# Network two, six steps of sevens: the read of the spare bank stands ahead of a gate, block 21 is bent later in one form of step, and a sum's split moves to the next step

## The chip, the cores and the metric

The kernel is one program on one core of a Trainium2 chip. The metric is the device time of one launch in microseconds (us); smaller is better. The kernel before takes 1674.57 us, the median of three runs between 1674.49 and 1675.16 us. The profile is one more execution, which took 1676.13 us; the trace of it covers a span of 1674.1 us.

## The reference

Three stages, all in float32: the real part of a two-dimensional Fourier transform of x (4 x 3072 x 256), a gated channel mix with squared ReLU (network one, 1024 hidden channels), and then network two, in which the change lies:

```python
def _moe2_ref(x, w_in, w_out):        # x: 12288 x 256, w_in: 256 x 2048, w_out: 2048 x 256
    h = x @ w_in
    g = h - np.tanh(h)
    return (g @ w_out).astype(np.float32)
```

## The kernel before, in words

**Precision.** TensorE multiplies a reduced float type here, so every operand is split into a high and a low part, and each product of a block is three matmuls (`mm3`, lines 395 to 397: high by high, high by low, low by high). The high part is a cast on ACT (`hi`, line 1082), the low part a subtraction (`lo`, line 1084) on DVE or on POOL.

**Tiling of network two.** The 12288 tokens are 12 passes of two token blocks of 512. The 2048 hidden channels are eight groups, q = 0 to 7, of two blocks of 128. One `step(n, q)` computes, for pass n and group q, the four blocks 11, 12, 21, 22 (128 x 512 each) of h, bends each (`bend`: tanh on ACT into a buffer `c`; then the "gate", a subtraction on DVE, gives g), and multiplies them by w_out. Pass 0 has another routine; passes 1 to 11 are 88 calls of `step`.

**Sevens.** The first matrix is done by seven products instead of eight for each step (the names a11, a12, s2, s3, s1, a22, s4 are the operands). They are accumulated in PSUM banks: X (two banks that alternate from step to step), Z, and W. Products that overlap in a bank are read off one after the other: Z begins as an ACT copy of X (line 1111, `z<-x` in the trace), takes a12, is bent and gated, then is overwritten by DVE with W plus the saved s3 (line 1191), bent by t22, gated (line 1208), and cast to the operand a22 (line 1082); X takes a22 at the end and is bent (t21). The second matrix is done by sevens too in the steps q = 0, 1, 3, 4, 6 and 7 (in pass 11 not in 7), and plainly, block by block, in q = 2 and 5. A step of sevens needs sums of its g blocks (s1, s2, s3, s4), which DVE and POOL make and which are split like the rest.

**The second matrix is late.** A step makes its operands while the next one or two steps run: `late(...)` runs pieces that the previous step (`p1`) left. What it can do depends on whether the previous step and the one before it were of sevens: form "b" if both were (q = 0, 1, 2, 5), "e" if only the previous was (q = 4, 7, and step (1,1)), "c" if the previous was not (q = 3, 6). So a pass runs b b b c e b c e.

**The spare bank.** Sums over several groups (a11, s1, s2, s3) are collected by `apart` in the bank X that this step does not use, called K; `add` then reads K on DVE into an accumulator `acc` in SBUF (lines 1028 and 1030). Two groups are read together where one follows the other. K is the previous step's X, so its first matmul comes after the last DVE read of that X (the low part of s1, `ls1`, line 1084 `s<-x,s`), and it is the next step's X, so the next step's first product comes after the read of K. Each step with a pair has two reads: one after the a11 cast, one (`k2`) after the gate of block 22.

**The order.** All engines run their instructions in program order; the order is the one in which `step` is written, and nothing else plans it. On ACT the tail of a step of form c or e stands as: tanh of Z (t22), tanh of X (t21, if the step is of sevens), cast of a22, and then, from the next step, the copy of block 22 to SBUF (`g22`, line 1235), the copy `z<-x`, and so on. Pass outputs of the pass before are made in steps 0, 1 and 3 by `part` (line 1045, DVE) and `whole_out` (line 1055, POOL). The stream of w_in (`TI`, 896 KB a step) and the stores go through SP's queue.

Of the kernel before, what the change touches and what calls it, by code (L numbers as in the profile page):

```python
# [406 lines left out]
class Kernel:  # L407
# [650 lines left out]
    def step(self, n, q):  # L1058

        V, A, T, G = self.V, self.A, self.T, self.G  # L1060
        TANH = mybir.ActivationFunctionType.Tanh
        S, W = self.S2[n], self.TI.pop(8 * n + q)
        p1, p2, p3 = self.pend, self.older, self.oldest
        seven = q in self.sevens(n)
        one, two = (bool(p and p["seven"]) for p in (p1, p2))
        form = "b" if one and two else "c" if not one else "e"
        group = lambda p, o: [o, p] if p["q"] in (1, 4, 7) else [p]
        def P(ps, k, start=False):
            i = RIGHT[k]
            mm3(T, ps, [W[:, 0, i], W[:, 1, i]], [S[k][:, 0], S[k][:, 1]], start)  # L1070
        def bend(src):
            t = self.room(self.act, "c", "c", 4)
            A.activation(t, src, TANH)  # L1073
            return t
# [4 lines left out]
        M, st = {}, {}  # L1079
        def hi(k, src):  # L1080
            M[k] = self.operand(k, *self.span(n, q, k))
            A.copy(M[k][:, 0], src)  # L1082
        def lo(k, src, eng):
            eng.tensor_sub(M[k][:, 1], src, M[k][:, 0].bitcast(F32))  # L1084
        late = lambda *names: [p1["late"][k]() for k in names]
# [12 lines left out]
        X, Z = self.bank(f"x{self.odd}", "x"), self.bank("z", "z")  # L1098
# [62 lines left out]
        add = k1() if k1 else nop  # L1161
# [15 lines left out]
        if not side:  # L1177
            lo("a11" if seven else "11", Z, V)
        if form == "b":
            late("hs2", "ls2")  # L1180
        elif form == "e":
            late("hs4", "ls4")
# [3 lines left out]
        add = k2() if k2 else nop  # L1186
# [5 lines left out]
        t22 = bend(Z)  # L1192
        if form == "b":
            late("hs4", "ls4")
        elif form == "e":
            late("hs2", "ls2")
        if q == 1 and n > 1:
            self.part(n - 1, 0, 1)
            self.whole_out(n - 1, 0, 1)
        if q == 0 and n > 1:  # L1200
            self.part(n - 1, 1, 0)
        if (n, q) == (1, 1):
            self.part(0, 0, 0)
        self.fill()
        if seven:
            P(X, "a22")
            st["t21"] = bend(X)
        V.tensor_sub(Z, Z, t22)  # L1208
        hi("a22" if seven else "22", Z)
        if seven and one:  # L1210
            V.tensor_sub(X, X, st["t21"])
        add()
        if (n, q) == (1, 1):
            self.part(0, 0, 1)
        if q == 1 and n > 1:
# [3 lines left out]
        if q == 3 and n > 1:  # L1219
            self.whole_out(n - 1, 1, 1)  # L1220
        self.fill()
        if not seven:
            P(X, "a22")
        P(Wb, "s4")
        def t21():
            st["t21"] = bend(X)
# [5 lines left out]
        if seven:  # L1232
            def f22():
                st["22"] = new("g22")
                A.copy(st["22"], Z)
            def g12():
                st["12"] = new("g12")
                V.tensor_sub(st["12"], Wb, st["t12"])
            def S4():
                st["12"] = new("g12")  # L1240
                V.tensor_sub(st["12"], Wb, st["22"])
            g = lambda k: st[k]
            do.update({
                "l22": lambda: lo("a22", Z, V), "f22": f22,
                "s3": lambda: V.tensor_sub(g("11"), g("11"), X), "s1": lambda: V.tensor_add(X, X, g("22")), "g12": g12,  # L1245
                "+s2": lambda: G.tensor_sub(g("22"), g("22"), g("11")), "+s4": lambda: G.tensor_sub(g("12"), g("12"), g("22")),  # L1246
                "G12": lambda: V.tensor_sub(Wb, Wb, st["t12"]), "S4": S4,
                "hs1": lambda: hi("s1", X), "ls1": lambda: lo("s1", X, V), "hs3": lambda: hi("s3", g("11")), "ls3": lambda: lo("s3", g("11"), G),
                "ha12": lambda: hi("a12", g("12") if "12" in st else Wb), "la12": lambda: lo("a12", g("12"), G), "LA12": lambda: lo("a12", Wb, V),
                "hs2": lambda: hi("s2", g("22")), "ls2": lambda: lo("s2", g("22"), G),  # L1250
                "hs4": lambda: hi("s4", g("12")), "ls4": lambda: lo("s4", g("12"), G)})
            w = self.W7[q]
        else:
            do.update(g12=lambda: V.tensor_sub(Wb, Wb, st["t12"]), h21=lambda: hi("21", X), l21=lambda: lo("21", X, V),
                      h12=lambda: hi("12", Wb), l12=lambda: lo("12", Wb, V))
            w = [[self.WO[q][:, s, 256 * c:256 * c + 256] for s in range(2)] for c in range(2)]
        self.oldest, self.older = p2, p1
        self.pend = dict(n=n, q=q, m=M, w=w, late=do, seven=seven)

# [4 lines left out]
    def phase2(self):  # L1264
        A, V = self.A, self.V
        z0 = 16 * NP
        self.W7, self.C, self.acc, self.older, self.oldest = {}, {}, {}, None, None
        self.at(z0 + 28, lambda: self.stream(8))
        self.TI = dict(enumerate(self.TI))
        for j in range(3, 8):  # L1270
            self.weights2(z0 + 4 * (j - 2), j, self.kp, "xt", 4)
        xt, wf, ring = (self.kp, "xt", 4), (self.p2a, "wf", 1), (self.w1, "T", 4)
        t4 = (lambda: self.p2b, lambda: self.p2a)
        for i, (q, slot, src) in enumerate(((0, 23, xt), (1, 26, xt), (3, 29, xt), (4, 38, wf), (6, 51, wf), (7, 56, wf))):
            self.seven(z0 + slot, q, *((self.p2a, f"TI{i}", 1) if i < 4 else ring), *src, t4[i % 2])
        for n in range(NP):
            for q in range(8):
                if n == 0 and q == 1:
                    self.xctx.close()
                    self.p2b = self.ctx.enter_context(self.tc.tile_pool(name="p2b", bufs=1, side="right", reuse_waits="tile"))  # L1280
                    self.homes = [[self.p2a, "WO0", 1, 1.5], [self.p2a, "WO1", 1, 2.5], [self.p2a, "WO3", 1, 4.5], [self.w1, "WR", 1, 0.], [self.p2b, "M", 2, 1.], [self.p2b, "M", 2, 1.1],
                                  [self.wvp, "wv", 4, 5.6], [self.wvp, "wv", 4, 7.6], [self.wvp, "wv", 4, 9.8]] + [[self.act, "m", 4, t] for t in (8.3, 8.6, 9.3, 9.8)]
                if q == 1 and n + 1 < NP:
                    u = self.left2(n + 1)
                    names = "a11 a12 a22 +s1 +s3 +s2 +s4 s1 s3 s2 s4".split()
                    when = (7, 8, 11, 12, 12, 15, 16, 16, 19, 20, 22) if n == 0 else (12, 12, 13, 14, 14, 15, 24, 24, 25, 26, 27)
                    self.at(z0 + 32 * n + (8 if n else 5), u["load"])
                    for k, name in zip(when, names):
                        self.at(z0 + 32 * n + k, u[name])
                if n:  # L1290
                    self.step(n, q)
                else:
                    w2 = [[self.WO[q][:, s, 256 * c:256 * c + 256] for s in range(2)] for c in range(2)]
                    self.quad(2, n, q, 8, self.S2[n], self.TI.pop(q), w2, None)
                if (n, q) == (NP - 1, 3):
                    self.at(self.now + 1, *self.plain(7))
            if n == 0:
                self.pend["seven"] = False
                self.C.update({(0, t, h): self.O[t][h] for t in range(2) for h in range(2)})
        p, w, n, G = self.pend, self.older, NP - 1, self.G  # L1300
        late = lambda *names: [p["late"][k]() for k in names]
        a11, h, s2, t = (self.acc[n, k] for k in ("a11", "h", "s2", "t"))
        self.direct(w, "a12")
        K = self.bank(f"x{1 - self.odd}", "k")
        L = self.bank("z", "l")
        def extra(ps, k):
            a, m = self.product(w, k)
            mm3(self.T, ps, a, [m[:, 0], m[:, 1]])
        extra(K, "s2")
        late("t21", "c12")  # L1310
        V.tensor_add(s2, s2, K)
        V.tensor_add(t, t, K)
        late("t12", "g21")
        G.tensor_add(s2, s2, h)
        self.whole(p, "11")
        extra(L, "s3")
        late("h21", "g12", "l21", "h12", "l12")
        V.tensor_add(t, t, L)
        self.whole(p, "22")
        G.tensor_add(h, h, t)  # L1320
        self.direct(w, "s4")
        V.tensor_add(t, t, a11)
        self.whole(p, "21")
        for k, (i, a) in enumerate((((1, 0), t), ((1, 1), h), ((0, 0), a11), ((0, 1), s2))):
            if k == 2:
                self.whole(p, "12")
            V.tensor_add(a, a, self.C.pop((n, *i)))
            self.send(n, *i, a, True)
# [118 lines left out]
```

## Time and profile before

| | |
|---|---|
| median of three runs | 1674.57 us (1674.49 to 1675.16) |
| profiled execution, device time | 1676.13 us |
| its span in the trace | 1674.1 us |
| PE (TensorE) busy | 1620.0 us, 97%, 7283 matmuls |
| DVE busy | 1356.0 us, 81% |
| ACT busy | 1273.7 us, 76% |
| POOL busy | 1112.9 us, 66% |
| network two, passes 1 to 11 | from about 742 us to the end |

A matmul here has a modelled end, so "busy" for PE says that the queue was full, and the count of matmuls in a stretch says how fast it ran. Idle time of an engine counts only where the engine that ends the stretch waits for it. In a row of the timeline the columns are: start (us from the span's start), duration, engine, line of the kernel, operation, output and inputs, shapes, and, in brackets, how long the engine had been idle before it and the instruction whose end released it.

### The profile page before, as it was taken

To read this page: it belongs to the slowest core of one execution; us is meant where nothing else is said; L and a number is where in the kernel's file an instruction comes from. 1 tells how busy PE (TensorE), PEld (TensorE's weight loads), DVE (VectorE), ACT (ScalarE), POOL (GpSimd) and SP (SyncE) were. 2 spreads that over 40 slices of the span, in tenths; PEclk is the share of its full clock that TensorE was granted. 3 is DMA by queue.
4 is the path that set the end of the run, shared out by engine and by line. 5 is a ranking of instruction groups with operands and counts; after the bars stand their busy time and mean duration, and the time that the engine had idled before them with its cause. 6 is when DMAs were issued, how large, how long until landed. Compare 5 with 4: busy or idle time off the path is not lost.

```text
span 1674.1 us, 22514 instructions
## 1 busy us (share of the span) xinstructions
PE 1620.0 (97%) x7283; PEld 1298.5 (78%) x7283; DVE 1356.0 (81%) x2115; ACT 1273.7 (76%) x2464; POOL 1112.9 (66%) x928
## 2 busy tenths in 40 slices
PE   8999999999999999999999999999999999999998
PEld 7978878888888887877777777777777777777776
DVE  7987888888888887777777777777787777778777
ACT  5987777777777777877878777777777777787774
POOL 1166667676666666768876767676767676767663
PEclk9999999999999999999999999999999999999999
DMA  9620111101111133443242424242424242424240
GB/s 333 169 58 26 46 45 64 34 30 57 53 57 63 45 107 105 160 159 143 73 134 93 132 95 132 95 132 95 133 94 133 91 136 89 139 88 138 89 141 26
DMA packets 59350, 168.76 MB, mean 101 GB/s; under 512 B 6864, under 2 KB 15824, under 8 KB 59232
## 3 DMA queue, kind: packets, MB, share of 16 engines
q1 hardware_dynamic: 57648, 162.87, 28.7%
q0 software_dynamic: 1440, 4.46, 1.6%
q8 instruction: 57, 0.93, 0.2%
q14 instruction: 61, 0.50, 0.1%
q10 hardware_dynamic: 144, 0.00, 0.0%
HBM read 128.43 MB, written 38.86 MB: 100 GB/s over the span
## 4 chain that ended last, share of the span: by engine, by line
PE 35%; ACT 10%; DVE 8%; issue 1%; DVEq 0%; POOLq 0%; ACTq 0%
PE x L395 4%; PE k L395 4%; PE k L397 3%; PE k L396 3%; PE x L397 3%; PE x L396 3%; ACT c L1073 3%; PE o L395 3%; PE o L397 3%; PE o L396 3%; ACT s L1082 3%; DVE a L1084 2%; ACT a L1082 2%; PE w L395 2%; PE w L397 1%; PE w L396 1%
## 5 line engine op out<-in xcount | busy, mean ns | idle before, releaser
L1084 POOL TENSOR_TENSOR s<-g,s 128x512 fp32r<-128x512 f32 x195 | 251.6, 1298 | 14.4 <-ACT s L1082 12.8
L1246 POOL TENSOR_TENSOR g<-g,g 128x512 f32<-128x512 f32 x107 | 138.6, 1296 | 118.8 <-DVE x L1245 73.2
L696 POOL TENSOR_TENSOR s<-xk,s 128x512 fp32r<-128x512 f32 x94 | 125.0, 1331 | 102.2 <-ACT s L694 97.7
L696 POOL TENSOR_TENSOR a<-xk,a 128x512 fp32r<-128x512 f32 x70 | 92.3, 1328 | 123.3 <-ACT a L694 123.2
L396 PE MATMUL o<-m,wv 128*128 128x512 f32 x384 | 149.6, 390 | 0.0
L397 PE MATMUL o<-m,wv 128*128 128x512 f32 x384 | 149.5, 389 | 0.0
L395 PE MATMUL o<-m,wv 128*128 128x512 f32 x384 | 149.5, 389 | 0.0
L1073 ACT ACTIVATE c<-z 128x512 f32<-128x512 f32 x176 | 105.3, 598 | 42.5 <-DVE z L1191 41.4
L1082 ACT CAST s<-g 128x512 fp32r<-128x512 f32 x195 | 120.8, 620 | 5.9 <-DVE g L1245 5.9
L1077 ACT COPY s<-x 128x512 f32<-128x512 f32 x176 | 103.9, 590 | 24.6 <-PE x L397 22.2
L1084 DVE TENSOR_TENSOR a<-z,a 128x512 fp32r<-128x512 f32 x108 | 74.3, 688 | 48.6 <-ACT a L1082 41.0
L571 ACT ACTIVATE c<-z 128x512 f32<-128x512 f32 x112 | 67.3, 601 | 54.8 <-DVE z L660 54.5
L578 DVE TENSOR_TENSOR m<-z,m 128x512 fp32r<-128x512 f32 x112 | 76.8, 686 | 33.4 <-ACT m L576 33.4
L1111 ACT COPY z<-x 128x512 f32<-128x512 f32 x88 | 50.2, 570 | 65.8 <-PE x L397 30.0
L1208 DVE TENSOR_TENSOR z<-z,c 128x512 f32<-128x512 f32 x88 | 61.6, 700 | 46.4 <-ACT c L1073 44.7
L395 PE MATMUL x<-a,TI 128*128 128x512 f32 x192 | 77.0, 401 | 17.2 <-DVE acc L1030 16.9
L430 POOL TENSOR_TENSOR xr<-xt,xr 128x512 fp32r<-128x512 f32 x46 | 60.5, 1322 | 48.3 <-ACT xr L429 48.3
L1084 POOL TENSOR_TENSOR a<-g,a 128x512 fp32r<-128x512 f32 x64 | 83.1, 1299 | 12.0 <-ACT a L1082 9.8
L576 ACT CAST m<-z 128x512 fp32r<-128x512 f32 x112 | 65.9, 589 | 29.9 <-DVE z L664 25.4
L396 PEld LDWEIGHTS o<-m,wv 128*128 128x128 f32 x384 | 72.1, 188 | 15.6 <-DVE m L578 0.5
L395 PEld LDWEIGHTS o<-m,wv 128*128 128x128 f32 x384 | 72.1, 188 | 15.2
L397 PEld LDWEIGHTS o<-m,wv 128*128 128x128 f32 x384 | 72.1, 188 | 15.1
(1020 smaller groups left out, 5824.6 us busy)
## 6 DMA issues: line engine op xcount, KB each, us to landing
TI<-ti SPq DMA_DIRECT2D x88, 896.0 KB, 4.8
spill<-r SPq DMA_DIRECT2D x48, 256.0 KB, 2.6
xk<-spill SPq DMA_DIRECT2D x48, 256.0 KB, 6.5
out<-o SPq DMA_DIRECT2D x44, 256.0 KB, 2.4
ti<-TI SPq DMA_DIRECT2D x8, 896.0 KB, 4.8
wf<-wf SPq DMA_DIRECT2D x17, 256.0 KB, 2.9
raw<-w_in SPq DMA_DIRECT2D x32, 128.0 KB, 2.2
cv<-w_out SPq DMA_DIRECT2D x16, 256.0 KB, 3.2
```

The costliest lines, as they stand in the source:

```text
L395: T.matmul(ps, w[0], m[0], start=start, stop=False, skip_group_check=True)
L396: T.matmul(ps, w[0], m[1], start=False, stop=False, skip_group_check=True)
L397: T.matmul(ps, w[1], m[0], start=False, stop=stop, skip_group_check=True)
L571: A.activation(t, src, ACT.Tanh if ph == 2 else ACT.Relu)
L576: A.copy(M[blk][:, 0], g)
L578: V.tensor_sub(M[blk][:, 1], g, M[blk][:, 0].bitcast(F32))
L696: eng.tensor_sub(S[name][:, 1], src(), S[name][:, 0].bitcast(F32))
L1073: A.activation(t, src, TANH)
L1077: A.copy(t, src)
L1082: A.copy(M[k][:, 0], src)
L1084: eng.tensor_sub(M[k][:, 1], src, M[k][:, 0].bitcast(F32))
L1246: "+s2": lambda: G.tensor_sub(g("22"), g("22"), g("11")), "+s4": lambda: G.tensor_sub(g("12"), g("12"), g("22")),
```

## The change

Four edits in `step` and what goes with it; the number of instructions on each engine stays the same.

1. The read of K (`add`, the second one of a step) stands ahead of the gate of block 22, and the pass outputs `part`/`whole_out` of steps 0 and 1, which stood ahead of that gate, stand behind the gates.
2. In form c, a step of sevens now runs its last product P(X, "a22") and the bend of block 21 after the cast of a22 (as plain steps do); in forms b and e the order of the two stays.
3. In form e the split of the previous step's sum s2 (`hs2` on ACT, `ls2` on POOL) is not run; it is kept in `self.slow`, and the next step, of form b, runs it just ahead of its own `hs2`, `ls2`. After the last step it is run at the beginning of the tail.
4. The loading of w_out's sevens for group 4 is set two slots later (40 for 38), once in the program.

```diff
         if form == "b":
+            if self.slow:
+                self.slow["late"]["hs2"]()
+                self.slow["late"]["ls2"]()
             late("hs2", "ls2")
         elif form == "e":
             late("hs4", "ls4")
...
         t22 = bend(Z)
         if form == "b":
             late("hs4", "ls4")
-        elif form == "e":
-            late("hs2", "ls2")
+        if (n, q) == (1, 1):
+            self.part(0, 0, 0)
+        self.fill()
+        early = seven and form != "c"
+        if early:
+            P(X, "a22")
+            st["t21"] = bend(X)
+        add()
+        V.tensor_sub(Z, Z, t22)
+        hi("a22" if seven else "22", Z)
+        if seven and one:
+            V.tensor_sub(X, X, st["t21"])
         if q == 1 and n > 1:
             self.part(n - 1, 0, 1)
             self.whole_out(n - 1, 0, 1)
         if q == 0 and n > 1:
             self.part(n - 1, 1, 0)
-        if (n, q) == (1, 1):
-            self.part(0, 0, 0)
-        self.fill()
-        if seven:
-            P(X, "a22")
-            st["t21"] = bend(X)
-        V.tensor_sub(Z, Z, t22)
-        hi("a22" if seven else "22", Z)
-        if seven and one:
-            V.tensor_sub(X, X, st["t21"])
-        add()
...
         self.fill()
-        if not seven:
+        if not early:
             P(X, "a22")
+            if seven:
+                st["t21"] = bend(X)
         P(Wb, "s4")
...
+        self.slow = p1 if form == "e" else None
         self.oldest, self.older = p2, p1
...
-        for i, (q, slot, src) in enumerate((... (4, 38, wf), ...)):
+        for i, (q, slot, src) in enumerate((... (4, 40, wf), ...)):
...
         a11, h, s2, t = (self.acc[n, k] for k in ("a11", "h", "s2", "t"))
+        self.slow["late"]["hs2"]()
+        self.slow["late"]["ls2"]()
         self.direct(w, "a12")
```

What the edits do to the order of the instructions is shown at four places. First, DVE at the end of a step of form c (pass 3, step 3); `z<-w,s` is line 1191 that overwrites Z, `z<-z,c` the gate of block 22, `acc<-k` the read of K, `a<-z,a` the low part of a22. Before:

```order
L1191 TENSOR_TENSOR z<-w,s 128x512
L1208 TENSOR_TENSOR z<-z,c 128x512
L1028 COPY acc<-k 128x512
L1084 TENSOR_TENSOR a_9499<-z,a_9499 128x512
L1228 TENSOR_TENSOR w<-w,s 128x512
L1231 TENSOR_TENSOR x<-x,c 128x512
```

and after:

```order
L1194 TENSOR_TENSOR z<-w,s 128x512
L1028 COPY acc<-k 128x512
L1206 TENSOR_TENSOR z<-z,c 128x512
L1084 TENSOR_TENSOR a_9496<-z,a_9496 128x512
L1232 TENSOR_TENSOR w<-w,s 128x512
L1235 TENSOR_TENSOR x<-x,c 128x512
```

The read of K and the gate have changed places; nothing else moved there on DVE.

Second, ACT at the same place and into the next step, of form e (pass 3, steps 3 and 4); `c<-z` is t22, `c<-x` is t21, `a<-z` the cast of a22, `g<-z` the copy of block 22. Before:

```order
L1073 ACTIVATE c<-z 128x512
L1073 ACTIVATE c<-x 128x512
L1082 CAST a_9499<-z 128x512
L1235 COPY g_9517<-z 128x512
L1111 COPY z<-x 128x512
L1073 ACTIVATE c<-w 128x512
```

and after:

```order
L1073 ACTIVATE c<-z 128x512
L1082 CAST a_9496<-z 128x512
L1073 ACTIVATE c<-x 128x512
L1239 COPY g_9517<-z 128x512
L1111 COPY z<-x 128x512
L1073 ACTIVATE c<-w 128x512
```

The tanh of X has moved behind the cast of a22.

Third, ACT at the end of a step of form e and the start of the next, of form b (pass 3, steps 4 and 5); `s_9584` is the high part of the second sum s2 of step 3. Before:

```order
L1082 CAST s_9571<-g_9551 128x512
L1073 ACTIVATE c<-z 128x512
L1082 CAST s_9584<-g_9517 128x512
L1073 ACTIVATE c<-x 128x512
L1082 CAST a_9593<-z 128x512
L1235 COPY g_9609<-z 128x512
L1111 COPY z<-x 128x512
```

and after, where the same cast has the name `s_9661` and stands later, in step 5 (the second piece):

```order
L1082 CAST s_9571<-g_9551 128x512
L1073 ACTIVATE c<-z 128x512
L1073 ACTIVATE c<-x 128x512
L1082 CAST a_9590<-z 128x512
L1239 COPY g_9606<-z 128x512
L1111 COPY z<-x 128x512
...
L1077 COPY s<-x 128x512
L1082 CAST s_9661<-g_9517 128x512
L1082 CAST s_9664<-g_9606 128x512
L1073 ACTIVATE c<-z 128x512
```

One cast has left the stretch between the tanh of Z and the tanh of X.

Fourth, DVE at the end of a step of form b (pass 7, step 0); `o<-acc,o` is the pass output of line 1045, `x<-x,c` the gate of block 21, `g<-g,x` the sum s3 of the next step. Before:

```order
L1191 TENSOR_TENSOR z<-w,s 128x512
L1045 TENSOR_TENSOR o<-acc,o_11628 128x512
L1208 TENSOR_TENSOR z<-z,c 128x512
L1211 TENSOR_TENSOR x<-x,c 128x512
L1030 TENSOR_TENSOR acc<-acc,k 128x512
L1084 TENSOR_TENSOR a_12414<-z,a_12414 128x512
L1245 TENSOR_TENSOR g_12382<-g_12382,x 128x512
```

and after:

```order
L1194 TENSOR_TENSOR z<-w,s 128x512
L1030 TENSOR_TENSOR acc<-acc,k 128x512
L1206 TENSOR_TENSOR z<-z,c 128x512
L1209 TENSOR_TENSOR x<-x,c 128x512
L1045 TENSOR_TENSOR o<-acc,o_11628 128x512
L1084 TENSOR_TENSOR a_12413<-z,a_12413 128x512
L1249 TENSOR_TENSOR g_12379<-g_12379,x 128x512
```

The read of K has gone from behind both gates to ahead of them, and the pass output from ahead of the gates to behind them.

## Rows read from the trace of the kernel before

**Rows 1.** The profile's first line.
```profile
span 1674.1 us, 22514 instructions
```

**Rows 2.** Windows: window, PE, PEld, DVE, ACT, POOL, PEclk, DMA, GB/s.
```profile
400.00:500.00 100.00, 100.00 (x441) 82.18 (x441) 88.89 (x131) 75.88 (x141) 68.11 (x55) 1.00 0.14 46
...
733.00:1650.00 917.00, 880.55 (x3712) 683.39 (x3710) 725.03 (x1127) 713.79 (x1336) 654.66 (x522) 1.00 0.33 111
```

**Rows 3.** Waits of PE, 742 to 1660: sum, count, longest (us).
```profile
PE x L395 <- DVE acc L1030: 16.9, 20, 1.3
PE z L395 <- ACT z L1111: 11.4, 23, 1.1
PE k L395 <- DVE s L1084: 6.7, 22, 1.8
```

**Rows 4.** Timeline, pass 5, end of step 3 (c) into step 4 (e).
```profile
1108.16 0.70 DVE L1208 TENSOR_TENSOR z<-z,c 128x512 f32<-128x512 f32 x1 [0.67 <-ACT c L1073]
...
1108.77 0.68 DVE L1028 COPY acc<-k 128x512 f32<-128x512 f32 x1
...
1110.19 0.60 ACT L1073 ACTIVATE c<-x 128x512 f32<-128x512 f32 x1 [2.07 <-PE x L397]
...
1110.68 0.58 ACT L1082 CAST a<-z 128x512 fp32r<-128x512 f32 x1
...
1111.07 0.39 PE L397 MATMUL x<-a,TI 128*128 128x512 f32 x1
...
1111.30 0.69 DVE L1084 TENSOR_TENSOR a<-z,a 128x512 fp32r<-128x512 f32 x1 [1.85 <-ACT a L1082]
...
1112.02 0.59 ACT L1235 COPY g<-z 128x512 f32<-128x512 f32 x1 [0.76 <-DVE a L1084]
...
1112.64 0.57 ACT L1111 COPY z<-x 128x512 f32<-128x512 f32 x1
...
1113.27 0.50 PE L395 MATMUL z<-a,TI 128*128 128x512 f32 x1 [0.45 <-ACT z L1111]
```

**Rows 5.** Timeline, pass 5, step 4 (e) into step 5 (b).
```profile
1117.12 0.19 PEld L395 LDWEIGHTS w<-s,TI 128*128 128x128 f32 x1 [0.30 <-DVE g L1241]
...
1119.42 0.61 ACT L1082 CAST s<-g 128x512 fp32r<-128x512 f32 x1
...
1119.55 0.70 DVE L1208 TENSOR_TENSOR z<-z,c 128x512 f32<-128x512 f32 x1 [0.66 <-ACT c L1073]
...
1120.41 0.59 ACT L1082 CAST a<-z 128x512 fp32r<-128x512 f32 x1
...
1121.52 0.69 DVE L1084 TENSOR_TENSOR a<-z,a 128x512 fp32r<-128x512 f32 x1 [0.27 <-ACT g L1235]
...
1124.82 0.50 PE L395 MATMUL k<-a,W 128*128 128x512 f32 x1 [0.24 <-DVE s L1084]
```

**Rows 6.** Timeline, pass 6, steps 0 to 1 to 2 (b).
```profile
1160.07 0.68 DVE L1045 TENSOR_TENSOR o<-acc,o 128x512 f32<-128x512 f32 x1
...
1160.28 2.56 POOL L1084 TENSOR_TENSOR s<-g,s 128x512 fp32r<-128x512 f32 x2
...
1163.17 0.68 DVE L1084 TENSOR_TENSOR a<-z,a 128x512 fp32r<-128x512 f32 x1
...
1163.31 0.50 PE L395 MATMUL x<-a,TI 128*128 128x512 f32 x1 [0.65 <-DVE acc L1030]
...
1164.30 0.57 ACT L1111 COPY z<-x 128x512 f32<-128x512 f32 x1 [1.40 <-PE x L397]
...
1165.20 1.30 POOL L1246 TENSOR_TENSOR g<-g,g 128x512 f32<-128x512 f32 x1 [2.37 <-DVE x L1245]
...
1165.93 0.69 DVE L1084 TENSOR_TENSOR s<-x,s 128x512 fp32r<-128x512 f32 x1 [0.28 <-ACT s L1082]
...
1166.84 0.40 PE L395 MATMUL k<-s,W 128*128 128x512 f32 x1
...
1177.70 0.40 PE L395 MATMUL k<-a,W 128*128 128x512 f32 x1
```

More of the change, by code (lines that the diff above doesn't have):

```diff
@@ L1266, in phase2 @@
         z0 = 16 * NP
-        self.W7, self.C, self.acc, self.older, self.oldest = {}, {}, {}, None, None
+        self.W7, self.C, self.acc, self.older, self.oldest, self.slow = {}, {}, {}, None, None, None
         self.at(z0 + 28, lambda: self.stream(8))
@@ L1273, in phase2 @@
         t4 = (lambda: self.p2b, lambda: self.p2a)
-        for i, (q, slot, src) in enumerate(((0, 23, xt), (1, 26, xt), (3, 29, xt), (4, 38, wf), (6, 51, wf), (7, 56, wf))):
+        for i, (q, slot, src) in enumerate(((0, 23, xt), (1, 26, xt), (3, 29, xt), (4, 40, wf), (6, 51, wf), (7, 56, wf))):
             self.seven(z0 + slot, q, *((self.p2a, f"TI{i}", 1) if i < 4 else ring), *src, t4[i % 2])
```

## The prediction

> **What bounds the kernel now.** I read the page's first line, then windows, then the waits of PE, and last the timeline at three places. The span is 1674.1 us [rows 1]; the device time of that execution is 1676.13, so 2.0 us lie outside the span and stay. The windows [rows 2] say how full TensorE is (granted clock 1.00 in both stretches, the level of 2.4 GHz): in a dense stretch of network one 441 matmuls pass in 100 us, 0.227 us each. In passes 1 to 11 of network two 3712 pass in 917 us; at 0.227 they would need 842. So TensorE waits there for up to 75 us, while DVE, ACT and POOL are busy for 725, 714 and 655 of the 917: no engine is full, the chains between them set the end. The list of waits [rows 3] names three kinds: X's first product waits for the read of K (16.9 us in 20), Z's first product for the copy `z<-x` (11.4 in 23), K's first product for the low part of s1 (6.7 in 22), 35.0 us together. The matmul that waited is listed with 0.50 us, the others with 0.39 [rows 4]: 0.11 of restart, 65 times, 7.2 us. So 42 us hang on the three waits, and each edit points at one of them.
>
> **c to e (edits 1 and 2 together).** In [rows 4] the gate of block 22 runs at 1108.16, the read of K behind it at 1108.77, but the cast of a22 only at 1110.68: ACT first bends X (t21, 1110.19), which waits for X's last product. Then follow one after the other the low part (1111.30), the copy of block 22 (1112.02), `z<-x` (1112.64), and Z's first product at 1113.27. It had 0.45 idle ahead of it; the matmul before it ended at 1112.82, so began at 1112.43, and 1112.65 was possible. After the change the gate comes a DVE slot later, at 1108.77, and ends at 1109.47 (0.70 as now); the cast starts at 1109.5, 1.17 earlier than now, since t21 no longer stands ahead of it. The low part follows at 1110.13 and the block's copy at 1110.86 (steps of 0.62 and 0.72, as in the rows). `z<-x` would follow at about 1111.50, when X's product is there (its last matmul runs from 1111.07 to 1111.46), and ends at 1112.07, ahead of 1112.65. So the wait goes, 0.62 and the restart. More hangs on this Z: the bend of block 11, its gate, the cast and low part of block 12 and the sum for which `w<-s` waited at 1117.12 [rows 5]. That comes about 1.0 earlier, at 1116.12.
>
> **e to b (edit 3).** Here K's first product waits for s1, at 1124.82 with 0.24 idle [rows 5]. Backwards its chain is the low part of a22 (1121.52, held by ACT's copy of block 22), the cast of a22 (1120.41), and ahead of it on ACT t21 and the cast of s2 (1119.42, 0.61 long). With Z's chain 1.0 earlier and that cast gone from ACT, the gate (1119.55 now, 1118.55 then) is what the cast of a22 waits for: 0.70 on, at 1119.25, 1.16 earlier. I carry 1.11 on, since ACT must first end t21: the low part comes at 1120.41 instead of 1121.52. What follows on DVE up to the low part of s1 moves with it, and K's first product starts at 1123.71, 1.11 earlier. That is all of what c to e gave and a little more, one gain for each c, e, b and not a sum of two. Of the 22 waits of K one lies in the tail; the 21 others get the gain in full (23.3 us). The first e, step (1,1), has no such wait behind it and pass 0's outputs in it; I give it 0.8. Together **24.1 us**.
>
> The cast and POOL's subtraction of s2 move into the next b step, 0.6 of ACT and 1.3 of POOL. There POOL stands idle 2.37 us ahead of its next sum (at 1165.20, [rows 6]), which hides it, and the products that use s2 come a step later. Behind pass 11 nothing hides it: the 1.2 that K's last wait loses is given back by 1.30 of POOL ahead of the tail's first s2. I take 0; from -1.3 to +1.3 is possible.
>
> **b to b to b (edit 1).** X's first product waits for the read of K (1163.31, 0.65 idle, [rows 6]); by [rows 3] the mean of the 20 is 0.85. The read moves ahead of the gate, so this wait goes. But DVE's work is the same five instructions: pass output (1160.07 to 1160.75), gate, block 21's gate, read of K, low part of a22 (1163.17). In the new order the read can start about where the pass output ends now, 1160.8; two gates and the pass output follow in slots of 0.6, and the low part is at 1163.2 as before. `z<-x`, which waited for X (1164.30), follows the low part's end, at 1163.9. Behind it ACT's casts of s3 and s1 wait for sums on DVE that have not moved, so that s1's low part comes at 1165.73 instead of 1165.93. K's first product, without a wait at 1166.84 now, would be reached by TensorE at 1165.9 and must wait for s1 till 1166.47, with 0.11 of restart. An x wait of 0.9 turns into a k wait, and 0.26 is gained. In the next step, by the same working, 1177.70 becomes 1177.13. I take 0.55 a pass, **5.5 us** in ten. The ends: 0 if s1 doesn't move, and 16.9 + 20 x 0.11 = 19 if K's product waits for nothing.
>
> In the plain steps 2 and 5 the gate, too, is a slot of 0.61 later; their operands are used behind other products, and the waits listed [rows 3] have none on them. I take 0; at most 21 x 0.61 = 13 are lost. The later load (edit 4) is once in the program, half a pass ahead of its use: 0.
>
> Sum: 24.1 + 5.5 = 29.6, so 1676.13 - 29.6 = 1646.5 for an execution like the profiled one; its time lies 1.56 over the median of the runs, so **1645.0** for the median.
>
> One row speaks on a danger of edits 1 and 3, POOL's subtractions and the pass output beside each other. In [rows 6] the pass output, whose inputs are both in SBUF (1160.07, 0.68), lies beside two subtractions of POOL (1160.28, 2.56 for both): DVE takes 0.68 as in its other rows and POOL 1.28 each. By that the move costs nothing. The Trainium skill ("SBUF — State Buffer", section "Who interferes with whom") has it that DVE and GpSimd share a pair of SBUF ports under an exclusive lock. By that rule such pairs would take longer, which these rows don't show; what it would make of the time is the fourth rival.
>
> **The rivals.**
> 1. The three waits vanish and none takes their place: 42 less, **1632**. For it: no engine is busy over 79% of the stretch. Against it: in b steps s1's low part hangs on DVE instructions in series that the change doesn't shorten. Chance 0.12.
> 2. The gains are given back at the next wait: in b to b all, and in c to e all but the cast of s2 that leaves ACT's path (0.61, [rows 5]), because `z<-x` is held by X or the next step by block 12. Then 22 x 0.61 = 13: **1661**. For it: the end of X's product leaves `z<-x` only 0.04 of slack. Against it: each link of Z's chain stands back to back in [rows 4]. Chance 0.17.
> 3. Slower: the later gate decides. In all 65 steps with a second read of K (0, 1, 2, 3, 5, 6 of a pass) the gate moves back by 0.61. If K's products end later than the bend t22, as they do once TensorE waits at K, the read stands, and the gate, the cast, the block's copy and the low part are late by as much, and with them the next step's Z and s1. 65 x 0.61 = 39.7 lost against 24.1 won: **1690**. It decides from the point where Z's chain, not the bend of X on ACT, is the last thing that the next step's s1 waits for, in c as in b. Against it: in c the cast stands 1.2 behind the gate's end now (twice a slot). Chance 0.06.
> 4. POOL and DVE hold each other up where the subtraction of s2 now lies: 23 x 1.30 = 30 lost against 29.6 won, **1675**. Against it the rows of 0.68 and 2.56 above. Chance 0.02.
>
> **How the numbers follow.** The forecast has 0.63, the rivals 0.12, 0.17, 0.06, 0.02. About 0.2%, 3.3 us, is what a measurement of this kernel can tell from no change. The forecast's own bounds go from 1631.5 (b to b 19 in place of 5.5) to 1659 (plain steps 13 and the tail 1.3 lost). With rivals 1 and 2 and their spread the range for 8 in 10 is 1631 to 1664; most of rivals 3 and 4 and the edges are left out. Faster by over 0.2%: the forecast and rivals 1 and 2, 0.92, less 0.01 of the second's tail: 0.91. No change: that 0.01 and rival 4, 0.03. Slower: 0.06.
>
> **What would show it.** In the trace after: no wait of X on the read of K worth 2 us in the list, waits of Z on `z<-x` under a third of 11.4; about 42 waits of K on s1 in place of 22, over 10 us in sum; in form c the cast of a22 right behind its gate and ahead of t21; K's first product in steps 1 and 2 a little over 10.8 apart, as now (1166.84 to 1177.70); POOL at 1.30 and DVE at 0.69 as before. The prediction is wrong if Z's waits stay at 11 us, if the cast of a22 in form c starts over 0.3 behind its gate's end, if the b steps come out longer, or if K's waits add up to as much as X's and Z's gave back.

## The result, and the profile after

The changed kernel takes 1648.32 us (median of four runs, 1647.95 to 1648.92) against 1674.53 for the kernel before in the same comparison: ratio 0.9844, 95% interval 0.9827 to 0.9861. That is 26.2 us, 1.56%. The forecast was 1645.0.

The profiled execution took 1648.92 us. The first line of its page, and its windows with the columns of [rows 2]:

```profile
span 1647.1 us, 22505 instructions
...
400.00:500.00 100.00, 100.00 (x442) 82.22 (x441) 88.87 (x131) 75.33 (x141) 68.16 (x54) 1.00 0.14 46
733.00:1625.00 892.00, 872.89 (x3720) 686.86 (x3719) 730.88 (x1132) 728.40 (x1341) 654.78 (x524) 1.00 0.34 114
```

The dense stretch of network one is the same, and the granted clock is. Network two now passes 3720 matmuls in 892 us where it passed 3712 in 917; at 0.227 us each they would need 844, so at most 48 us are not filled where it was 75.

The waits of PE after (sum, count, longest, in us), to be held against [rows 3]:

```profile
PE k L395 <- DVE s L1084: 6.4, 22, 1.4
PE o L396 <- POOL s L1084: 5.3, 10, 0.6
PE o L395 <- DVE o L1045: 4.5, 10, 0.7
PE z L395 <- ACT z L1111: 1.0, 1, 1.0
PE w L395 <- DVE g L1245: 0.9, 1, 0.9
PE k L396 <- POOL s L1084: 0.8, 1, 0.8
```

The 16.9 us of X behind the read of K are gone, and 22 of the 23 waits of Z. Two kinds are new in the list, 10 each: a product into an output bank (`o`) that waits for POOL's low part of a sum, and one that waits for the pass output of line 1045. The list leaves out waits of about 0.1 us and less, and one new kind is among these: K's first product in step 2 (below).

**c to e.** The timeline of the changed kernel where [rows 4] stood before (pass 5, end of step 3):

```profile
1097.31 0.69 DVE L1028 COPY acc<-k 128x512 f32<-128x512 f32 x1 [0.61 <-PE k L397]
...
1097.92 0.69 DVE L1206 TENSOR_TENSOR z<-z,c 128x512 f32<-128x512 f32 x1
...
1098.64 0.59 ACT L1082 CAST a<-z 128x512 fp32r<-128x512 f32 x1 [1.31 <-DVE z L1206]
...
1099.26 0.69 DVE L1084 TENSOR_TENSOR a<-z,a 128x512 fp32r<-128x512 f32 x1 [0.65 <-ACT a L1082]
...
1099.35 0.60 ACT L1073 ACTIVATE c<-x 128x512 f32<-128x512 f32 x1
...
1099.98 0.59 ACT L1239 COPY g<-z 128x512 f32<-128x512 f32 x1
...
1100.71 0.57 ACT L1111 COPY z<-x 128x512 f32<-128x512 f32 x1
...
1101.81 0.39 PE L395 MATMUL z<-a,TI 128*128 128x512 f32 x1
```

The gate comes a slot behind the read, the cast 0.72 after the gate's start, and the tanh of X behind the cast. Z's first product has 0.39, not 0.50, and no idle time: it waited for nothing.

**e to b.** Where [rows 5] stood (pass 5, steps 4 and 5):

```profile
1105.34 0.50 PE L395 MATMUL w<-s,TI 128*128 128x512 f32 x1
...
1107.76 0.70 DVE L1206 TENSOR_TENSOR z<-z,c 128x512 f32<-128x512 f32 x1 [0.67 <-ACT c L1073]
...
1108.49 0.59 ACT L1082 CAST a<-z 128x512 fp32r<-128x512 f32 x1 [0.18 <-DVE z L1206]
...
1109.60 0.69 DVE L1084 TENSOR_TENSOR a<-z,a 128x512 fp32r<-128x512 f32 x1 [0.54 <-ACT g L1239]
...
1112.90 0.50 PE L395 MATMUL k<-a,W 128*128 128x512 f32 x1 [0.24 <-DVE s L1084]
```

The cast waits for the gate now. From `w<-s` to the low part of a22 it is 4.26 us; before it was 1121.52 - 1117.12 = 4.40 [rows 5]. K still waits 0.24 for s1, earlier by all that its step won.

**b to b to b.** Where [rows 6] stood (pass 6, steps 0 to 2):

```profile
1147.22 3.79 POOL L1084 TENSOR_TENSOR s<-g,s 128x512 fp32r<-128x512 f32 x3
...
1149.57 0.68 DVE L1045 TENSOR_TENSOR o<-acc,o 128x512 f32<-128x512 f32 x1
...
1150.17 0.68 DVE L1084 TENSOR_TENSOR a<-z,a 128x512 fp32r<-128x512 f32 x1
...
1151.07 0.50 PE L396 MATMUL o<-s,W 128*128 128x512 f32 x1 [0.51 <-POOL s L1084]
...
1153.74 0.39 PE L395 MATMUL k<-s,W 128*128 128x512 f32 x1
...
1161.12 0.47 PE L395 MATMUL o<-s,W 128*128 128x512 f32 x1 [0.42 <-DVE o L1045]
...
1164.18 0.19 PEld L395 LDWEIGHTS k<-a,W 128*128 128x128 f32 x1 [0.51 <-DVE s L1084]
...
1164.18 0.50 PE L395 MATMUL k<-a,W 128*128 128x512 f32 x1
```

The three subtractions of POOL in one row (the moved one is the first) end at 1151.01, and the second matmul of a direct product waits for the last of them. In the next step the first matmul of the same product waits for the pass output, which stands behind the gates now. Between the two, K's first product in step 1 waits for nothing (0.39). In step 2 it waits for the low part of s1: its weight load names it, the matmul has 0.50, and its idle time is 0.09. So it is in each of passes 2 to 11, which makes 32 waits of K on s1 where the list shows 22.

A table by step, made from the start of each `z<-x` copy to the next (mean of passes 2 to 11, us), shows where the time came from:

| from step | 0 | 1 | 2 | 3 (c to e) | 4 | 5 | 6 (c to e) | 7 | pass |
|---|---|---|---|---|---|---|---|---|---|
| before | 10.58 | 10.89 | 9.59 | 12.13 | 9.65 | 9.66 | 12.06 | 9.72 | 84.28 |
| after | 10.23 | 10.76 | 9.67 | 11.14 | 9.68 | 9.69 | 10.91 | 9.67 | 81.75 |

Two intervals give 2.1 of the 2.5 us of a pass, both from a c step into an e step.

### The profile page after: what moved, and what is told of

It is laid out like the page before. It is cut to its first block, busy times and chain, and to the rows that moved or that the text cites. A ratio compares the mean times of both kernels' runs of the same rounds, so it can differ in the third digit from the quotient of the medians.

```text
span 1647.1 us, 22505 instructions
## 1 busy us (share of the span) xinstructions
PE 1610.7 (98%) x7283; PEld 1301.4 (79%) x7283; DVE 1356.9 (82%) x2115; ACT 1285.9 (78%) x2464; POOL 1110.5 (67%) x928
## 4 chain that ended last, share of the span: by engine, by line
PE 35%; ACT 8%; DVE 7%; POOL 2%; issue 2%; DVEq 0%; POOLq 0%; ACTq 0%
PE k L395 3%; ACT s L1082 3%; PE o L396 3%; PE o L397 3%; PE o L395 3%; PE k L396 3%; PE k L397 3%; PE x L397 3%; PE x L395 3%; PE x L396 3%; PE w L395 2%; POOL s L1084 2%; DVE a L1084 2%; PE w L397 1%; PE w L396 1%
## 5 line engine op out<-in xcount | busy, mean ns | idle before, releaser
L1030 DVE TENSOR_TENSOR acc<-acc,k 128x512 f32<-128x512 f32 x86 | 59.1, 687 | 44.1 <-PE k L397 44.1
L576 ACT CAST m<-z 128x512 fp32r<-128x512 f32 x112 | 65.9, 589 | 27.5 <-DVE z L664 23.0
L1082 ACT CAST a<-z 128x512 fp32r<-128x512 f32 x108 | 64.0, 593 | 29.5 <-DVE z L1206 27.3
```

The lines of the kernel that those rows point to most:

```text
L576: A.copy(M[blk][:, 0], g)
```

## The experiments

All were run against the kernel before on one chip for each of three groups; ratios are to it. "Interval 3" is the column 3 of the table above, and differences of intervals are to the changed kernel, mean of passes 2 to 11.

| kernel | us, median | ratio, 95% interval |
|---|---|---|
| the change | 1648.32 | 0.9844 (0.9827 to 0.9861) |
| no_read | 1651.59 | 0.9859 (0.9846 to 0.9873) |
| no_late21 | 1669.20 | 0.9963 (0.9951 to 0.9976) |
| no_slow | 1648.73 | 0.9843 (0.9830 to 0.9856) |
| twice | 1679.42 | 1.0024 (1.0013 to 1.0034) |
| split_last | 1650.96 | 0.9853 (0.9833 to 0.9873) |
| outputs | 1647.24 | 0.9825 (0.9808 to 0.9843) |
| read_b_only | 1646.22 | 0.9822 (0.9806 to 0.9838) |
| three | 1644.19 | 0.9811 (0.9795 to 0.9827) |
| pool_last | 1645.29 | 0.9821 (0.9807 to 0.9834) |
| three_b | 1641.64 | 0.9799 (0.9786 to 0.9812) |
| s3_first | 1656.63 | 0.9890 (0.9877 to 0.9904) |
| four | 1645.97 | 0.9825 (0.9812 to 0.9839) |

### no_read: the change without edit 1

```diff
-        add()
+        if q == 1 and n > 1:
+            self.part(n - 1, 0, 1)
+            self.whole_out(n - 1, 0, 1)
+        if q == 0 and n > 1:
+            self.part(n - 1, 1, 0)
         V.tensor_sub(Z, Z, t22)
         hi("a22" if seven else "22", Z)
         if seven and one:
             V.tensor_sub(X, X, st["t21"])
-        if q == 1 and n > 1:
-            self.part(n - 1, 0, 1)
-            self.whole_out(n - 1, 0, 1)
-        if q == 0 and n > 1:
-            self.part(n - 1, 1, 0)
+        add()
```

> The change without edit 1: the read of K stands behind the gates again, and the pass outputs of steps 0 and 1 ahead of the block-22 gate. Theory: only the steps b to b to b lose, about 0.4 us a pass (what the intervals 0 to 2 of the changed kernel gained over before), so 1648.3 + 4 = 1652, with about 17 us of waits of X on the read of K back in the list and the new waits of the direct products on POOL and on the pass output gone: 1650 to 1655. Rival: the read's place is worth its whole wait of 17 us and restarts, 1667. Second rival: the gate, now a slot earlier in 65 steps, gives back more than it loses, below 1646.

Measured: 1651.59. The first lines of its waits of PE:

```profile
PE x L395 <- DVE acc L1030: 16.9, 20, 1.3
PE k L395 <- DVE s L1084: 6.4, 22, 1.4
```

X's wait is back to the tenth, 16.9 us, and yet only 3.3 us are lost: intervals 0 and 1 lose 0.35 and 0.13, interval 2 gains 0.08, and interval 3, a c step, gains 0.13. A wait of 17 us was worth about 4, because another one stood behind it; and in the c step q = 3 the later gate costs a tenth. In the other c step it costs nothing: interval 6 is 0.03 longer here.

### no_late21: the change without edit 2

```diff
-        early = seven and form != "c"
+        early = seven
```

> The change without edit 2: in form c block 21 is bent ahead of the cast of a22 again. Theory: the c to e wait of Z (0.62 and a restart) is back at 22 places and with it the 1.0 that the e step's chain had won; in the e to b step only 0.1 to 0.2 is left of the gain. 22 x 0.95 = 21 lost: 1669 (1665 to 1672). Rival: the s2 cast that left ACT in the e step is worth 0.5 to 0.6 by itself, so only 22 x 0.5 = 11 to 13 are lost: 1660.

Measured: 1669.20. Two lines of its waits, the first of them the wait of Z:

```profile
PE z L395 <- ACT z L1111: 10.7, 22, 1.1
...
PE k L395 <- DVE s L1084: 4.9, 21, 0.2
```

Intervals 3 and 6 are 1.12 and 1.11 longer, 4 and 7 shorter by 0.14 and 0.08. So the tanh of X that moved behind one cast (with X's last product) carries 21 of the 26 us. The theory's number held, and the rival's 1660 did not.

### no_slow: the change without edit 3

```diff
         if form == "b":
-            if self.slow:
-                self.slow["late"]["hs2"]()
-                self.slow["late"]["ls2"]()
             late("hs2", "ls2")
...
             late("hs4", "ls4")
+        elif form == "e":
+            late("hs2", "ls2")
```

(and without the two calls in the tail)

> The change without edit 3: the split of s2 stays in the e step and nothing is moved into the b step or the tail. Theory: with Z's chain earlier by 1.0, the cast of a22 in the e step waits for its gate and hardly for the s2 cast and t21; 0.1 to 0.16 us at 21 places are lost, 2 to 3.4, and in the b step the wait of the direct product on POOL (5.3 us in 10) goes, of which K's wait for s1 leaves 0.2 to 0.3 each, 2 to 3, and the tail gets back up to 1.2: 1648.3 within 2. Rival: the s2 cast is what gives the e to b gain, as its 0.61 on ACT suggests: 1648.3 + 13 = 1661.

Measured: 1648.73. Two lines of its waits:

```profile
PE k L395 <- DVE s L1084: 8.8, 32, 1.4
PE o L395 <- DVE o L1045: 4.4, 10, 0.7
```

POOL's wait is gone and ten more of K's have come, as the theory had it. Intervals 4 and 7 are longer by 0.12 and 0.13, interval 1 shorter by 0.15: edit 3 is worth nothing that can be measured here, since what it gives in two steps POOL takes back in one and in the tail.

### twice: the gate of block 22 in two instructions

```diff
         add()
-        V.tensor_sub(Z, Z, t22)
+        if k2:
+            V.tensor_sub(t22, Z, t22)
+            V.tensor_copy(Z, t22)
+        else:
+            V.tensor_sub(Z, Z, t22)
```

> The change with the block-22 gate made in two DVE instructions (subtraction into the bend's buffer, then a copy back to Z) in the 65 steps with a second read of K: the cast of a22 comes one DVE slot, 0.6 to 0.7, later, the result is the same. Theory: form c has just that much slack (z<-x at 1112.07 against 1112.65), so c to e loses 0.1 at 22 places; the b steps 0 and 1 have the low part of a22 straight on the path through s1 and K and lose 0.6 each, 12; plain steps nothing: 1648.3 + 14 = 1662 (1656 to 1668). Rival, the later gate decides everywhere: 65 x 0.65 = 42, 1690. Rival, there is slack everywhere: 1649.

Measured: 1679.42, a miss between the theory and its rival. Intervals 0, 2, 3, 5 and 6 are longer by 0.63, 0.72, 0.62, 0.70 and 0.37, and 1 by 0.18; 4 and 7 are shorter by 0.15 and 0.22. Steps 2 and 5 are plain; I had them free. What ended ACT's idle time ahead of `z<-x` (the group of that line, with its idle time in all and the releasers), in the kernel before, in the change, and here:

```profile
L1111 ACT COPY z<-x 128x512 f32<-128x512 f32 x88 | 50.2, 570 | 65.8 <-PE x L397 30.0 <-DVE a L1084 18.1 <-DVE w L1228 17.0
```

```profile
L1111 ACT COPY z<-x 128x512 f32<-128x512 f32 x88 | 50.2, 570 | 47.1 <-DVE a L1084 37.1 <-PE x L397 7.7 <-DVE 22_16150 L1084 0.3
```

```profile
L1111 ACT COPY z<-x 128x512 f32<-128x512 f32 x88 | 50.2, 570 | 42.9 <-DVE a L1084 34.2 <-PE x L397 1.1 <-DVE 22_14297 L1084 0.3
```

Before, X's product released most of that idle time. In the change the low part of a22 already does, that is, the gate's chain: in the steps 0, 1, 2 and 5. X's product is left with 7.7 us, in steps 3 and 6, behind the plain ones. With one slot more X hardly does it (1.1 us); the low part of block 22 stands there in its place, as `22_14297` in the row shows for one of them. So behind the plain steps the change had used up the room of about one slot: the first slot cost at most 0.08 there, the second 0.7. Over all 65 steps the second cost 30 us, 0.47 each; the first had cost 0.12 in step 3 and hardly anything in steps 2, 5 and 6 (read_b_only, below); in steps 0 and 1 no run shows it by itself.

### split_last and pool_last: the moved split behind that of s4

split_last moves both halves behind `late("hs4", "ls4")` in form b and keeps the split of the last e step there (the tail has none); pool_last leaves ACT's cast in its place and moves POOL's half alone:

```diff
             if self.slow:
                 self.slow["late"]["hs2"]()
-                self.slow["late"]["ls2"]()
             late("hs2", "ls2")
...
             late("hs4", "ls4")
+            if self.slow:
+                self.slow["late"]["ls2"]()
+        elif (n, q) == (NP - 1, 7):
+            late("hs2", "ls2")
```

> The change with the moved split of s2 put behind the split of s4 in the b step, and kept in the last e step, so that the tail has none. Theory: POOL's row of three subtractions (3.79 us) no longer ends behind the need of the direct product with s4; that wait (5.3 us and 10 restarts) goes, and K's wait for s1 comes up in its place at 0.25 to 0.35 each, as in the kernel without edit 3: 1.5 gained in step 1, 1.2 in the tail: 1645.6 (1644 to 1647). Rival: the wait is gone for good, 1648.3 - 6.4 - 1.2 = 1640.7. Rival: POOL is just as late for another product, 1647 to 1648.

Measured: 1650.96, worse than expected. Interval 1 is 0.20 shorter, but interval 0 is 0.41 longer. The timeline of ACT in step 0 (pass 6) shows the moved cast in the row of two between the two bends:

```profile
1146.58 0.60 ACT L1073 ACTIVATE c<-z 128x512 f32<-128x512 f32 x1 [0.44 <-DVE z L1191]
...
1147.08 1.13 ACT L1082 CAST s<-g 128x512 fp32r<-128x512 f32 x2
...
1148.11 0.60 ACT L1073 ACTIVATE c<-x 128x512 f32<-128x512 f32 x1
```

It stands ahead of t21 and so ahead of the gate of block 21, behind which the pass output and the low part of a22 stand on DVE: the place between the two bends that edit 3 had just cleared in form e.

> As the version with the moved split behind that of s4, but only POOL's half of it (the low part of s2) goes there; ACT's cast stays where the change has it, ahead of the bend t22. In the version before, the cast stood on ACT between t22 and the cast of a22, and step 0 became 0.35 longer. Theory: that 0.35 goes, step 1 keeps its 0.15 gain, the tail its 1.1 to 1.2: 1648.3 - 1.5 - 1.2 = 1645.6. Rival: the 0.35 came from POOL's order, then as before, 1649 to 1651.

Measured: 1645.29, as expected. Interval 0 is unchanged against the change, interval 1 shorter by 0.19, and the list has no wait of `o` on POOL. The 0.4 came from ACT's cast.

### outputs, read_b_only and three

outputs puts the two pass outputs where DVE is idle for K:

```diff
+        if q == 1 and n > 1:
+            self.part(n - 1, 0, 1)
         add()                                  # the first read of the step
...
+        if q == 0 and n > 1:
+            self.part(n - 1, 1, 0)
         add()                                  # the second
         V.tensor_sub(Z, Z, t22)
...
         if q == 1 and n > 1:
-            self.part(n - 1, 0, 1)
             self.whole_out(n - 1, 0, 1)
-        if q == 0 and n > 1:
-            self.part(n - 1, 1, 0)
```

> The change with the two pass outputs of DVE out of the path: in step 0 back ahead of the read of K, where DVE is idle 0.56 us waiting for K; in step 1 ahead of the first read, idle 0.61. Theory: the low part of a22 comes 0.6 earlier in both steps; in step 0 the direct product still waits for POOL and nothing is gained, in step 1 the wait on the pass output (4.5 us and restarts) goes and K's next wait (0.25) with it: 10 x 0.6 = 6 gained, 1642 (1640 to 1644). Rival: in step 0, too, DVE's chain is what counts: 12 gained, 1636. Rival: the wait moves on to s1 at K, 1647.

Measured: 1647.24, a miss: interval 1 is 0.20 shorter, interval 0 by 0.05, 2.4 us in ten passes. The rival was nearer: its first two lines of waits are

```profile
PE k L395 <- DVE s L1084: 8.6, 32, 1.4
PE o L396 <- POOL s L1084: 5.7, 10, 0.8
```

The wait on line 1045 is gone, and K's wait on s1 in step 2 has grown in its place from 0.09 to 0.24, so that the list has ten more. In step 1 K still doesn't wait; POOL's wait stands ahead of it.

read_b_only reads K ahead of the gate in steps 0 and 1 only:

```diff
-        add()
+        first = seven and form == "b"
+        if first:
+            add()
         V.tensor_sub(Z, Z, t22)
...
+        if not first:
+            add()
```

> The change with the read of K ahead of the gate in steps 0 and 1 only (form b, sevens); in the plain steps and in form c the gate comes first again. Theory: the later gate costs 0.12 in a c step and 0.09 in a plain one, as the kernel without edit 1 was faster there: 11 x 0.12 + 21 x 0.05 = 2.3 gained, 1646 (1645 to 1647.5). Rival: these tenths were the free room that the next wait takes, 1648.3.

Measured: 1646.22. Interval 3 is 0.12 shorter, 2 by 0.02, 5 by 0.01, and 6 is 0.02 longer: the c step q = 3 gives 1.2 us back, the other c step and the plain steps nothing to speak of.

> All three of the above together. Theory: without POOL's wait in step 0 the low part of a22, 0.6 earlier, counts there as well: 1648.3 - 1.2 (tail) - 12 (steps 0 and 1) - 2.3 = 1633 (1630 to 1637). Rival, only the sum of the single gains: 1648.3 - 2.7 - 6 - 2.3 = 1637.3.

three has the first three edits together (with split_last's form of the split). Measured: 1644.19, not 1633: the sum of the single gains, less what ACT's cast costs in interval 0. There is no second gain in step 0.

### three_b, s3_first and four: how far K's wait can be moved

three_b is three with pool_last's form of the split.

> The three edits together with ACT's cast left where the change has it. Theory: step 0 loses the 0.3 that it had from the cast: 1644.2 - 10 x 0.3 = 1641 (1640 to 1643). Rival: K's first product waits for the low part of s1 in every b step and a b step can't be shorter than that chain: 1644.

Measured: 1641.64, as expected, and the fastest kernel of all; intervals 0 and 1 are 10.16 and 10.38. Its list of waits of PE, the first line:

```profile
PE k L395 <- DVE s L1084: 10.7, 42, 1.4
```

With the other waits taken away, 42 waits of K on s1 are left: the picture that the prediction drew for the change itself. (The list of pool_last shows 32; with the ten short ones of step 2, 0.09 each, it has all 42 as well.)

s3_first makes the sum s3 ahead of the low part of a22; four is that with three_b:

```diff
         if form == "b":
-            late("f22", "l22")
+            late("f22", "s3", "l22")
...
-            late("s3", "s1", "+s2", "hs3", "hs1", "c12", "t12")
+            late("s1", "+s2", "hs3", "hs1", "c12", "t12")
```

> The change with one more move: in form b the sum s3 is made on DVE ahead of the low part of a22 (which waits there for ACT's copy of block 22), so that s1 and its low part come a slot earlier. Theory, that K's waits are the end of a DVE chain of low part, s3, s1, c12, low part of s1: s1's low part comes 0.4 to 0.6 earlier, K's waits of 0.51 with restart go in steps 0 and 5 (21), and half of the smaller ones: 1648.3 - 9 = 1639 (1636 to 1642), with the waits on POOL and on the pass output as large as before. Rival: ACT's order (z<-x, cast of s3, cast of s1) holds the low part of s1, and less than 3 us are gained: 1646.

> That move with the three edits (ACT's cast left in its place). Theory: with all four, the waits of K in steps 0, 1, 2 and 5 shrink from 0.51 each to 0.1 or nothing: 1641 - 41 x 0.4 = 1625 (1621 to 1631). Rival: a wait of another product comes up in each of these steps, 1636 or more.

Measured: 1656.63 and 1645.97, both slower than without the move (by 8.3 and 4.3): the theory fell, and the rival named the place, though not the size (1646). The timeline of s3_first (pass 6, step 1 into 2): s3, the low part of a22, the copy of Z, and the low part of s1.

```profile
1163.45 0.68 DVE L1249 TENSOR_TENSOR g<-g,x 128x512 f32<-128x512 f32 x1
...
1164.05 0.68 DVE L1084 TENSOR_TENSOR a<-z,a 128x512 fp32r<-128x512 f32 x1
...
1164.82 0.57 ACT L1111 COPY z<-x 128x512 f32<-128x512 f32 x1 [1.64 <-DVE a L1084]
...
1166.45 0.69 DVE L1084 TENSOR_TENSOR s<-x,s 128x512 fp32r<-128x512 f32 x1 [0.51 <-ACT s L1082]
```

The low part comes a slot later, `z<-x` waits for it (the two use bank Z), and the casts of s3 and s1 stand behind `z<-x` on ACT. So the low part of s1, which was to come earlier, waits 0.51 for its cast. DVE was ahead, ACT's order held it. K's first product still waits for it in steps 0, 1, 2 and 5, 0.08 to 0.10 each. What would happen with `z<-x` behind those casts was not tried.

## Why the prediction was right, point by point

**c to e.** It held step by step: the cast 0.72 behind the gate's start where 0.70 and a few hundredths were said, the low part 0.62 on, the block's copy 0.72 on, no wait for Z. `z<-x` came 0.73 behind the copy and not 0.64. The gain is 0.99 at step 3 and 1.15 at step 6 where 1.11 was said; no_read shows the missing tenth at step 3, 0.13: the gate's later slot isn't quite hidden there, while at step 6 it is.

**e to b.** That this is one gain and not two was the step on which the size hung, and it held: no_late21 lost 21 of the 24.1, no_slow nothing. Over a pass intervals 3 to 7 got shorter by 2.13 where 2.22 was said. The cast of s2, 0.61 long, was worth 0.12 to 0.14 by the intervals 4 and 7, as the gate was to become the later of the two.

**b to b to b.** The mechanism was half right. The read of K no longer stops X, and less than a quarter of the 16.9 us was won: 0.40 a pass where 0.55 was said, 0.35 + 0.13 in intervals 0 and 1, less 0.08 in 2. What was named to take its place, K's first product waiting for s1, came in step 2 and not in step 1. The step that failed is the sentence on the split, that POOL's idle 2.37 us hide it: this idle time lies behind the two subtractions of step 0, and the moved one stands ahead of them, so that the last of the three ends late for the direct product (5.3 us in 10). That was the missing part: no_slow and pool_last, without POOL's wait, have all 42 waits of K and won 0.53 and 0.59 in the three intervals. Nor did I see that the pass output, now late, holds an output bank that the next product needs (4.5 in 10). Two of the recorded signs failed with this: the list has 22 waits of K, 6.4 us, and not about 42 with over 10, and K's first products in steps 1 and 2 are 10.44 apart (1153.74 to 1164.18), not over 10.8. That last sign didn't fit its own working, which has 1166.47 and 1177.13, 10.66; and 1177.13 is 0.57 earlier, but with the restart of 0.11 that was taken off in the first step only 0.46 are gained, not 0.55.

**Plain steps, tail, rest.** In steps 2 and 5 I took 0 and bounded it by 13: the intervals behind them grew by 0.08 and 0.03 a pass, of which read_b_only gave back 0.02 and 0.01, and twice shows that the next slot there would have cost 0.7. In the tail the loss (from the last `z<-x` to the end 25.90 us, 24.55 before) is about what the interval ahead of it won (1.19), as said. The lines are POOL's wait of 0.8 in the list above and K's of 1.4, 1.8 before; no_slow, without edit 3, has 24.56. What lies ahead of the first `z<-x` took 0.8 less; in the runs of the variants it moved by -1.4 to +0.8 against the change, though none of them changes work there, so I put it down to no edit. Edit 4 is in every run, and the load that it moves lies in pass 1 (ACT's cast of it at 749.91 before, 755.38 after): it has no part in the means of passes 2 to 11, and what it is worth in pass 1 is not shown.

**The sum.** -0.8 ahead, -27.5 over the 87 intervals, +1.35 in the tail: -26.9, the spans' difference. Forecast 29.6. For the 24.1, intervals 3 to 7 won 21.4 (without the last 6, which the tail takes back) and the first three intervals of pass 1 0.95, where 0.8 was said for step (1,1): 22.3, 1.8 short. The tenth at step 3 is 1.2 of it; the rest is interval 7 of pass 1, 0.7 longer, in which the one wait of W (0.9 in the list above) lies. For the 5.5, intervals 0 to 2 of passes 2 to 11 won 4.0. The 0.8 ahead, which the forecast did not have, makes up for a little of that.

**The rivals.** That all waits vanish (1632) was wrong for the reason given, and three_b says how far: with all that was found taken away K's 42 waits remain. That the gains are given back (1661) is true of most of the 16.9 in b to b and of edit 3, not of c to e. That the later gate decides (1690) is false for this slot and true for the next: twice, at 1679.42, is slower than the kernel before. The fourth, of POOL and DVE holding each other up, is not borne out: POOL's rows stay at about 1.3 (3.79 for three), DVE's at 0.69. I must correct what I said beside it: one of the two inputs of line 1045 is the output bank in PSUM, so it is no instruction with two inputs in SBUF, and its row does not test that rule of the Trainium skill ("SBUF — State Buffer", section "Who interferes with whom"). The same section says that a DVE instruction with at most one SBUF input, outside the 2-port performance modes, does not contend with GpSimd; with that these rows agree (0.68 beside 1.28). The other case stands in network one of the kernel before, where line 824 reads two tiles in SBUF. Here it is alone, and beside a subtraction of POOL that began just ahead of it:

```profile
201.41 0.74 DVE L824 SCALAR_TENSOR_TENSOR xk<-xt,mut,y 128x512 f32<-128x512 f32 x1
...
204.64 1.29 POOL L696 TENSOR_TENSOR a<-xk,a 128x512 fp32r<-128x512 f32 x1 [7.04 <-ACT a L694]
204.70 1.78 DVE L824 SCALAR_TENSOR_TENSOR xk<-xt,mut,y 128x512 f32<-128x512 f32 x1
```

All 10 that begin so take 1.78, the 18 without POOL beside them 0.74 to 0.75. So the price that the fourth rival set exists in this kernel, about 1 us a pair, for two inputs in SBUF; each DVE instruction that was moved reads a bank in PSUM.

**The better version.** three_b, at 0.9799 (0.9786 to 0.9812), is faster than the change at 0.9844 (0.9827 to 0.9861). They ran on different chips, each against the kernel before.

## What to carry to other kernels

Where a chain of waits is cut at one link, the time that comes back is the distance to the next link, not the length of the wait: 16.9 us were worth 4 here, and one tanh behind one cast was worth 21, because everything that followed was in series with it. Look along each engine's order for an instruction that needs something late and stands ahead of one whose input is ready (t21 ahead of the cast of a22; the cast in split_last; `z<-x` in s3_first), and move it to a place where the engine is idle anyway. And before room is spent, double the spending once: a slot that costs nothing says nothing on the next one.

## What was not expected of the hardware

- One more DVE instruction of 0.7 us in 65 steps cost 30 us, 0.47 each, though DVE is busy for 731 of 892 us of the stretch; the first such slot had cost 0.12 in the steps q = 3 and next to nothing in q = 2, 5 and 6. Busy share says nothing of room in a chain.
- A matmul that waited is listed with 0.50 in place of 0.39, on whichever engine it waited for an operand, and the next one followed 0.34 later in place of 0.23 (1112.90 to 1113.24 in step 5 above). Behind the pass output it was 0.47 and 0.31. The ends of these rows are modelled; the start of the next matmul is not.
- A DVE instruction with two inputs in SBUF took 1.78 in place of 0.74 beside POOL (line 824, above).
